# Shifting the right-hand tiles by 320 bytes, moving sums of blocks to VectorE, and three more places for split blocks in a retention + two-MLP kernel

## Chip, cores and metric

The kernel runs on one core of one Trainium2 chip. The metric is the device time of one execution in microseconds; the median of three runs of the kernel before is 931.86 us (931.78 to 934.02).

## What is computed

Attention without softmax (retention), then two MLPs, all in float32:

```python
scores = q @ k.T / sqrt(64)                       # 4 batches, 8 heads, 576 positions, 64 wide
attn = (scores * gamma_h ** (i - j) for i >= j) @ v
x = attn as [2304, 512]
h = relu(x @ w_in)                                # 512 -> 2048   (MLP 1)
y = (h * h) @ w_out                               # 2048 -> 512
g = y @ w_gate                                    # 512 -> 1536   (MLP 2)
out = (g * sigmoid(g) * (y @ w_val)) @ w_out2     # 1536 -> 512
```

## The kernel before

Products of the MLPs are made to near float32 precision with TensorE's `float32r` type: each operand is split into a high part (a ScalarE copy that rounds) and a low part (a VectorE subtraction), and `three` (lines 174 to 178) issues high x high, high x low and low x high into one bank of PSUM. Each matmul has its own weight load.

**Order of the work.** Nothing is issued while the functions run. They describe operations with an engine, an estimated duration, their dependences and a rank to a planner (`Plan`, lines 59 to 119), which simulates the engines and issues, per engine, whichever operation is ready first; among ready ones the lowest rank goes first. TensorE's operations are chained in program order. Each engine then works its instructions off in the order issued. Stores have rank -4, loads of second-MLP weights -1, the evaluation of a step of the second MLP -3 and -2, attention about 10, conversion of first-MLP weights from 100 on, of second-MLP weights from 200 on.

**Stages.**
- Start: loads, attention cells 0 to 3; while data are awaited, `fill` (line 876) repeats a matmul whose two operands are one tile of zeros, `wz`, of the pool `hp`.
- MLP 1: tokens go in five blocks (`BLOCKS`, line 27), four of 512 columns and one of 256, each over 16 slices `f` of the hidden width. Per slice, 12 matmuls make `h` in one bank (`mlp1_h`), `mlp1_act` turns it into squares and splits it (relu and high part on ScalarE, square on ScalarE in the first and last block and on VectorE in the others, low part on VectorE, line 516), and 12 matmuls one slice later add to `y` in four banks (`mlp1_y`). Attention cells for the next block lie between slices. Meanwhile weights arrive as 64-bit words and are rounded to 32 bits (`round32`): those of MLP 1 during the first block, those of MLP 2 in later blocks, and the latter are stored, already split, in DRAM (`keep`).
- MLP 2: tokens in three blocks of 768, each over 12 slices; one of the 36 steps is seven products (a Strassen-Winograd scheme over 2 x 2 blocks, `PRODUCTS`, line 42), each of 6 matmuls of 384 columns into banks `MA` and `MB` alternately (tiles `gv`), and 18 output matmuls of 512 columns (lines 806 to 808). VectorE adds a product to partial sums before its bank is free again (lines 711 to 731; `u` of L731 is the last of a step, from which the next step's first product takes its bank).

**Sums of blocks.** The scheme needs sums of blocks of the weights and of y. `convert_gv` makes four sums of 256 columns for each of 12 gate/value slices (S1 to S4, line 295, GpSimd); `fetch_x` (line 606) loads one block's y into the tile `ys`, makes four differences of 768 columns (T1 to T4, line 621, GpSimd), and `part` splits seven blocks into tiles `xc` (ScalarE copy, line 252; VectorE subtraction, line 256). There are `NX` = 9 places for `xc`, so two of the next block's seven parts fit before the running block gives places free. The splits of a block are chained one after another (`x_chain`). The first block is fetched at rank 60, the next two at rank 4.

**Weights.** A ring place holds `P` (A11, A12, A22; 768 columns, high and low part 3072 bytes apart), `S` (S1 to S4; 1024 columns, 4096 apart) or `O` (output weights).

**Addresses.** Pools on the left are stacked upward, pools with `side="right"` downward from the top, the first of them a pad of 32 bytes (line 153). In the built program every tile that TensorE reads from a left pool (`x`, `h`, `wz`, attention tiles) starts 128 bytes past a multiple of 512 but for `state` (384 past); every tile of a right pool (all weights, `xc`, the split activations `at`, the tiles of the first attention cells) starts 448 past. All sizes between are multiples of 512.

Of the kernel before, what the change touches and what calls it, by code (L numbers as in the profile page):

```python
# [10 lines left out]
F32 = mybir.dt.float32  # L11
F32R = mybir.dt.float32r
# [3 lines left out]
ALU = mybir.AluOpType  # L16
# [12 lines left out]
T2, N2 = 6, 3  # L29
HALF = T2 * C // 2  # L30
# [10 lines left out]
         ("V", 1), ("raw", 1), ("A", 2), ("q", 2), ("V", 2), ("A", 3), ("q", 3), ("V", 3)]  # L41
PRODUCTS = [("A11", "B11"), ("A12", "B21"), ("S2", "T2"), ("S1", "T1"), ("S3", "T3"), ("S4", "B22"), ("A22", "T4")]
PLAIN, SUMS = ["A11", "A12", "A22"], ["S1", "S2", "S3", "S4"]
NX, NRING = 9, 7
INSERTS = {2: (4, 10), 4: (2, 6, 10, 13)}


# [90 lines left out]
def kernel(ctx: ExitStack, tc: tile.TileContext, units, qtab, tab, w1, w2, out):  # L138
# [10 lines left out]
    nc = tc.nc  # L149
    do = Plan()  # L150

    pad = ctx.enter_context(tc.tile_pool(name="pad", bufs=1, side="right"))
    pad.tile([128, 8], F32, name="pad")
    wp = ctx.enter_context(tc.tile_pool(name="wp", bufs=NW1 - NA, side="right"))
    wstack = ExitStack()
    wa = wstack.enter_context(tc.tile_pool(name="wa", bufs=NA, side="right"))
# [91 lines left out]
    def split(get, n, out, place, rank, deps, cols=None):  # L248

        def hi():  # L250
            out["t"] = place()
            nc.scalar.copy(out=out["t"][:, 0], in_=get())

        def lo():
            t = out["t"]
            nc.vector.tensor_tensor(out=t[:, 1], in0=get(), in1=t[:, 0].bitcast(F32), op=ALU.subtract)

        h = do("ACT", 0.17 + 0.43 * n / 512, hi, deps, rank)
        return do("DVE", 0.16 + 0.53 * n / 512, lo, [h], rank)
# [13 lines left out]
    def keep(kind, i, st, n, get, rank, deps):  # L273

        out = {}

        def store():
            nc.sync.dma_start(out=w_dram[kind, i], in_=out["t"].bitcast(F32))

        l = split(get, n, out, lambda: sp.tile([128, 2, n], F32R, tag="raw1", name="cw"), rank, [*deps, place_free[1]])  # L280
        w2_saved[kind, i] = place_free[1] = do("SP", 0.4, store, [l], rank - 100, kb=n)
        return l

    def convert_gv(box, f, rank):


        st, p4 = round32(box, rank)
        a21, a11, a12, a22 = (slice(256 * i, 256 * i + 256) for i in range(4))

        def add(i, a, b, op, new=False):  # L290
            def go():
                if new:
                    st["s"] = cv.tile([128, 4, 256], F32, tag="r", name="s")
                x, y = (st["s"][:, k] if isinstance(k, int) else st["fm"][:, k] for k in (a, b))
                nc.gpsimd.tensor_tensor(out=st["s"][:, i], in0=x, in1=y, op=op)
            return go

        s = do("POOL", 0.7, add(0, a21, a22, ALU.add, True), [p4], rank)
        s = do("POOL", 0.7, add(1, 0, a11, ALU.subtract), [s], rank)
        s = do("POOL", 0.7, add(2, a11, a21, ALU.subtract), [s], rank)  # L300
        s = do("POOL", 0.7, add(3, a12, 1, ALU.subtract), [s], rank)
        l = keep("P", f, st, 768, lambda: st["fm"][:, 256:], rank, [p4])
        f_users.append(do("NONE", 0.0, lambda: None, [s, l]))
        r_users.append(keep("S", f, st, 1024, lambda: st["s"].rearrange("p a b -> p (a b)"), rank, [s, l]))
# [5 lines left out]
    late, hps_free = {}, {}  # L310
# [291 lines left out]
    XC, As, ring = {}, {}, {}  # L602
    M_op, x_op, ld_op, o_op, g_op = (Named(do, k) for k in ("M", "xc", "ld", "o2", "g2"))
    steps2 = N2 * NF2

    def fetch_x(b, rank):

        st = {}

        def load():  # L610
            st["t"] = xp.tile([128, KC + 1, T2 * C], F32, tag="x", name="ys")
            nc.sync.dma_start(out=st["t"][:, :KC], in_=y_dram[b])

        def at(name):
            if name == "T2":
                return st["t"][:, KC].rearrange("p (k n) -> p k n", k=2)
            k, h = {"B11": (0, 0), "B12": (0, 1), "B21": (2, 0), "B22": (2, 1), "T1": (0, 0), "T3": (0, 1), "T4": (2, 0)}[name]
            return st["t"][:, k:k + 2, h * HALF:h * HALF + HALF]

        def sub(o, a, c):  # L620
            return lambda: nc.gpsimd.tensor_tensor(out=at(o), in0=at(a), in1=at(c), op=ALU.subtract)

        free = [h_op[NB - 2 + b, NF1 - 1]] if b < 2 else [("ysdone", b - 2)]
        ready = {}
        ld = do("SP", 0.4, load, [*y_saved[b], *free, late["open"]], rank, kb=1536)

        def part(i, name, deps):
            n = 7 * b + i
            old = M_op[((n - NX) // 7) * NF2 + NF2 - 1, (n - NX) % 7] if n >= NX else late["open2"]
            out = {}  # L630

            def place():
                XC[b, name] = late["xc"].tile([128, 2, 2, HALF], F32R, tag="xc", name="xc")
                return XC[b, name]

            x_op[b, i] = l = split(lambda: at(name), 2 * HALF, out, place, rank, [*deps, old, *x_chain[-1:]])
            x_chain.append(l)
            return l

        b11 = part(0, "B11", [ld])  # L640
        b21 = part(1, "B21", [ld])
        t1 = do("POOL", 1.95, sub("T1", "B12", "B11"), [b11], rank)
        t2 = do("POOL", 1.95, sub("T2", "B22", "T1"), [t1], rank)
        t3 = do("POOL", 1.95, sub("T3", "B22", "B12"), [t1], rank)
        t4 = do("POOL", 1.95, sub("T4", "B21", "T2"), [t2, b21], rank)
        part(2, "T2", [t2])
        part(3, "T1", [t1])
        part(4, "T3", [t3])
        part(5, "B22", [t3])
        do.named["ysdone", b] = part(6, "T4", [t4])  # L650

    x_chain = []
# [273 lines left out]
    def convert2():  # L926
        kind, f = todo.pop(0)
        i = NW2 - 1 - len(todo)
        box = load_raw(w2, i, 0, rank=200 + i)
        (convert_gv if kind == "gv" else convert_out)(box, f, 200 + i)  # L930
# [3 lines left out]
    for j in range(NB):  # L934
        more = BLOCKS[j + 1][1] if j + 1 < NB else 0
        at = dict(zip(INSERTS[more], range(cell, cell + more))) if more else {}
        cell += more
        if not more:
            def swap():
                astack.close()  # L940
                late["tl"] = ctx.enter_context(tc.tile_pool(name="tl", bufs=1, reuse_waits="tile"))
                pgv = ctx.enter_context(tc.tile_pool(name="pgv", bufs=1, space=PSUM, reuse_waits="tile"))
                late["MA"], late["MB"], more = (pgv.tile([128, 512], F32, name=f"gv{i}") for i in range(3))
                late["more"] = [banks[0], more]
                late["tp"] = tp

            def swap2():
                wstack.close()
                for key, bufs in (("xc", NX), ("rg", 1), ("at", 2), ("tm", 1)):
                    late[key] = ctx.enter_context(tc.tile_pool(name=key, bufs=bufs, side="right", reuse_waits="tile"))  # L950

            late["open"] = do("NONE", 0.0, swap, [*(x for xs_ in x_done.values() for x in xs_), *(st_op[c] for c in range(NC))])
            late["open2"] = do("NONE", 0.0, swap2, [late["open"], y_op[NB - 1, NA - 1]])
        for f in range(NF1):
            rank = 10 + f / 100
            if f == 1:
                for _ in range(LATER.get(j, 0)):
                    convert2()
            mlp1_h(j, f)
            mlp1_act(j, f)  # L960
            if pend:
                mlp1_y(*pend)
            pend = (j, f)
            if j == 0 and f == 1:
                att_scores(n0, rank)
            c = at.get(f)
            if c is not None:
                att_out(c, rank, "IKO", deps=[relu_op[j, f]])
                if c not in LAST:
                    hps_free[(j, f + 1) if f + 1 < NF1 else (j + 1, 0)] = [st_op[c]]  # L970
                if c + 1 < NC:
                    att_scores(c + 1, rank)
                if c + 1 < NC:
                    att_load(c + 1, 40)
# [4 lines left out]
    for s in range(steps2):  # L979
        b, f = divmod(s, NF2)  # L980
        mlp2_gv(s, last_y if s == 0 else () if s == 1 else mlp2_o(s - 2))
        if s == 0:
            fetch_x(0, 60)
        if f == 1 and b + 1 < N2:
            fetch_x(b + 1, 4)
    for s in (steps2 - 2, steps2 - 1):
        for piece in mlp2_o(s):
            piece()
# [69 lines left out]
```

## Time and profile before

| | before |
|---|---|
| median of three runs | 931.86 us (931.78 to 934.02) |
| the profiled execution, its own time | 934.56 us |
| its span, first to last instruction | 932.8 us |
| TensorE busy | 909.2 us |
| VectorE busy | 593.8 us |
| ScalarE busy | 362.3 us |
| GpSimd busy | 120.5 us |
| mean granted TensorE clock | 0.994 |

The rows come from one profiled execution. Times are from the span's start. PE is TensorE (PEld its weight loads), DVE VectorE, ACT ScalarE, POOL GpSimd, SP the queue that issues all transfers. Matmuls are pipelined: the duration of one runs on after the next has begun, so the pace is read from the distance of starts. A bracket behind a row holds the engine's idle time before it and what ended it.

### The profile page before, as it was taken

What the parts mean: (1) busy time and instruction counts of PE and PEld (TensorE: products, weight loads), DVE (VectorE), ACT (ScalarE), POOL (GpSimd) and SP (SyncE); (2) the same over time, 40 slices, a digit from 0 to 9 for tenths busy, and PEclk for the clock granted to TensorE, in tenths of its full rate; (3) what the DMA queues carried; (4) which work ended last, traced back from release to release, by engine and by line L of the source; (5) the groups of instructions that cost most, each with busy time, mean ns of one, the idle gap of its engine ahead of it and who ended that gap; (6) DMA issues with size and microseconds to landing.
All of it is one profiled execution on the core that took longest, in us unless ns stands there. A gap on an engine that the chain in (4) does not pass through costs nothing.

```text
span 932.8 us, 12545 instructions
## 1 busy us (share of the span) xinstructions
PE 909.2 (97%) x4953; PEld 793.7 (85%) x4953; DVE 593.8 (64%) x872; ACT 362.3 (39%) x546; POOL 120.5 (13%) x97
## 2 busy tenths in 40 slices
PE   8899999999999999999999999998999999999997
PEld 7688879988878778878887899998999999999996
DVE  5999836457773777736455655569655557655554
ACT  3678743234541445446553222223222223322221
POOL 3210102112431312301133000003000000000000
PEclk9999999999999999999999999999999999999999
DMA  8665605337673567645436754555555455745521
GB/s 350 226 208 185 227 36 185 123 109 265 236 260 102 177 232 296 226 173 220 181 131 250 297 207 188 219 203 203 199 222 209 187 225 207 277 187 224 208 115 68
DMA packets 36634, 187.49 MB, mean 201 GB/s; under 512 B 4192, under 2 KB 5984, under 8 KB 22624
## 3 DMA queue, kind: packets, MB, share of 16 engines
q1 hardware_dynamic: 36576, 186.70, 53.7%
q8 instruction: 39, 0.64, 0.3%
q14 instruction: 19, 0.16, 0.1%
HBM read 148.93 MB, written 37.75 MB: 200 GB/s over the span
## 4 chain that ended last, share of the span: by engine, by line
PE 88%; DVE 6%; DMA 2%; ACT 2%; issue 2%; SPq 0%; ACTq 0%; DVEq 0%
PE gv L178 9%; PE gv L177 9%; PE gv L176 9%; PE acc L177 7%; PE hps L176 7%; PE acc L176 7%; PE acc L178 7%; PE hps L178 6%; PE hps L177 6%; PE acc L807 4%; PE acc L808 4%; PE acc L806 3%; DMA raw<-w 2%; PE xs L427 2%; PE sc L390 2%
## 5 line engine op out<-in xcount | busy, mean ns | idle before, releaser
L176 PE MATMUL gv<-xc,w 128*128 128x384 f32 x504 | 170.2, 338 | 5.8 <-DVE u L731 3.4
L177 PE MATMUL gv<-xc,w 128*128 128x384 f32 x504 | 171.3, 340 | 0.0
L178 PE MATMUL gv<-xc,w 128*128 128x384 f32 x504 | 171.0, 339 | 0.0
L176 PE MATMUL acc<-h,w 128*128 128x512 f32 (+1 forms) x320 | 119.5, 373 | 2.9 <-ACT yt L573 2.2
L177 PE MATMUL acc<-h,w 128*128 128x512 f32 (+1 forms) x320 | 119.5, 373 | 2.6 <-DVE h L516 2.5
L176 PE MATMUL hps<-x,w 128*128 128x512 f32 (+1 forms) x320 | 120.8, 378 | 1.0 <-ACT r L503 1.0
L177 PE MATMUL hps<-x,w 128*128 128x512 f32 (+1 forms) x320 | 119.1, 372 | 0.9 <-DVE x L452 0.9
L178 PE MATMUL hps<-x,w 128*128 128x512 f32 (+1 forms) x320 | 119.0, 372 | 0.0
L178 PE MATMUL acc<-h,w 128*128 128x512 f32 (+1 forms) x320 | 118.9, 372 | 0.0
L176 PEld LDWEIGHTS gv<-xc,w 128*128 128x128 f32 x504 | 95.5, 189 | 15.7 <-DVE u L731 4.6
L177 PEld LDWEIGHTS gv<-xc,w 128*128 128x128 f32 x504 | 95.3, 189 | 8.2
L736 ACT ACTIVATE sg<-g 128x384 f32<-128x384 f32 x72 | 37.8, 525 | 162.9 <-DVE g L728 131.5
L178 PEld LDWEIGHTS gv<-xc,w 128*128 128x128 f32 x504 | 95.4, 189 | 0.0
L503 ACT ACTIVATE r<-hps 128x512 f32<-128x512 f32 (+1 forms) x80 | 44.4, 555 | 127.1 <-PE hps L178 116.9
L516 DVE TENSOR_TENSOR h<-r,h 128x512 fp32r<-128x512 f32 (+1 forms) x80 | 55.6, 695 | 59.5 <-ACT h L513 59.0
L176 PEld LDWEIGHTS acc<-h,w 128*128 128x128 f32 x320 | 60.1, 188 | 15.9 <-ACT yt L573 2.9
L177 PEld LDWEIGHTS acc<-h,w 128*128 128x128 f32 x320 | 60.1, 188 | 15.3 <-DVE h L516 4.1
L176 PEld LDWEIGHTS hps<-x,w 128*128 128x128 f32 x320 | 60.1, 188 | 14.8 <-ACT r L503 1.9
L177 PEld LDWEIGHTS hps<-x,w 128*128 128x128 f32 x320 | 60.2, 188 | 12.1 <-DVE x L452 1.2
L178 PEld LDWEIGHTS hps<-x,w 128*128 128x128 f32 x320 | 60.1, 188 | 11.5
L178 PEld LDWEIGHTS acc<-h,w 128*128 128x128 f32 x320 | 60.1, 188 | 11.4
L509 DVE TENSOR_TENSOR r<-r 128x512 f32<-128x512 f32 (+1 forms) x48 | 33.2, 692 | 48.2 <-ACT r L503 48.2
(106 smaller groups left out, 1486.6 us busy)
## 6 DMA issues: line engine op xcount, KB each, us to landing
w<-wdS SPq DMA_DIRECT2D x36, 1024.0 KB, 5.7
raw<-w SPq DMA_DIRECT2D x34, 1024.0 KB, 4.8
w<-wdP SPq DMA_DIRECT2D x36, 768.0 KB, 5.8
w<-wdO SPq DMA_DIRECT2D x18, 1024.0 KB, 4.8
wdS<-cw SPq DMA_DIRECT2D x12, 1024.0 KB, 4.2
wdP<-cw SPq DMA_DIRECT2D x12, 768.0 KB, 3.4
qk<-units SPq DMA_DIRECT2D x14, 512.0 KB, 4.4
kv<-units SPq DMA_DIRECT2D x14, 512.0 KB, 3.9
```

The costliest lines, as they stand in the source:

```text
L176: nc.tensor.matmul(ps, lhsT=wh, rhs=xh, start=first, stop=False)
L177: nc.tensor.matmul(ps, lhsT=wh, rhs=xl, start=False, stop=False)
L178: nc.tensor.matmul(ps, lhsT=wl, rhs=xh, start=False, stop=last)
L390: nc.tensor.matmul(s[h][:, p], lhsT=A[c][r, p, 1], rhs=A[c][r, p, 0], start=True, stop=True)
L427: nc.tensor.matmul(bank("xo")[r, p], lhsT=V[c][:, p, 1, r], rhs=P[c][:, h, p], start=c in FIRST and p == 0, stop=p == NP - 1)
L503: nc.scalar.activation(out=st["r"], in_=banks[0][:, :n], func=ACTF.Relu)
L509: nc.vector.tensor_tensor(out=st["r"], in0=st["r"], in1=st["r"], op=ALU.mult)
L516: nc.vector.tensor_tensor(out=Hs[j, f][:, 1], in0=st["r"], in1=Hs[j, f][:, 0].bitcast(F32), op=ALU.subtract)
L736: nc.scalar.activation(out=t, in_=st["g"][:, r], func=ACTF.Sigmoid)
L806: nc.tensor.matmul(ps, lhsT=at[:, 0, sl], rhs=wh, start=f == 0, stop=False)
L807: nc.tensor.matmul(ps, lhsT=at[:, 0, sl], rhs=wl, start=False, stop=False)
L808: nc.tensor.matmul(ps, lhsT=at[:, 1, sl], rhs=wh, start=False, stop=f == NF2 - 1)
```

## The change

The pad grows from 32 to 352 bytes, which moves every right-hand tile down by 320 bytes, from 448 to 128 past a multiple of 512. The sums S1 to S4 and the differences T1 to T4 are issued on VectorE. The places for `xc` become twelve, three of them in a new pool `xl` on the left (at 128 past as well), nine on the right as before. All blocks are fetched at rank 60, but the last two parts of the second and third block are split at rank 4.

```diff
--- before.py
+++ after.py
@@ -41,7 +41,7 @@
          ("V", 1), ("raw", 1), ("A", 2), ("q", 2), ("V", 2), ("A", 3), ("q", 3), ("V", 3)]
 PRODUCTS = [("A11", "B11"), ("A12", "B21"), ("S2", "T2"), ("S1", "T1"), ("S3", "T3"), ("S4", "B22"), ("A22", "T4")]
 PLAIN, SUMS = ["A11", "A12", "A22"], ["S1", "S2", "S3", "S4"]
-NX, NRING = 9, 7
+NX, NXL, NRING = 12, 3, 7
 INSERTS = {2: (4, 10), 4: (2, 6, 10, 13)}
 
 
@@ -150,7 +150,7 @@
     do = Plan()
 
     pad = ctx.enter_context(tc.tile_pool(name="pad", bufs=1, side="right"))
-    pad.tile([128, 8], F32, name="pad")
+    pad.tile([128, 88], F32, name="pad")
     wp = ctx.enter_context(tc.tile_pool(name="wp", bufs=NW1 - NA, side="right"))
     wstack = ExitStack()
     wa = wstack.enter_context(tc.tile_pool(name="wa", bufs=NA, side="right"))
@@ -292,13 +292,13 @@
                 if new:
                     st["s"] = cv.tile([128, 4, 256], F32, tag="r", name="s")
                 x, y = (st["s"][:, k] if isinstance(k, int) else st["fm"][:, k] for k in (a, b))
-                nc.gpsimd.tensor_tensor(out=st["s"][:, i], in0=x, in1=y, op=op)
+                nc.vector.tensor_tensor(out=st["s"][:, i], in0=x, in1=y, op=op)
             return go
 
-        s = do("POOL", 0.7, add(0, a21, a22, ALU.add, True), [p4], rank)
-        s = do("POOL", 0.7, add(1, 0, a11, ALU.subtract), [s], rank)
-        s = do("POOL", 0.7, add(2, a11, a21, ALU.subtract), [s], rank)
-        s = do("POOL", 0.7, add(3, a12, 1, ALU.subtract), [s], rank)
+        s = do("DVE", 0.43, add(0, a21, a22, ALU.add, True), [p4], rank)
+        s = do("DVE", 0.43, add(1, 0, a11, ALU.subtract), [s], rank)
+        s = do("DVE", 0.43, add(2, a11, a21, ALU.subtract), [s], rank)
+        s = do("DVE", 0.43, add(3, a12, 1, ALU.subtract), [s], rank)
         l = keep("P", f, st, 768, lambda: st["fm"][:, 256:], rank, [p4])
         f_users.append(do("NONE", 0.0, lambda: None, [s, l]))
         r_users.append(keep("S", f, st, 1024, lambda: st["s"].rearrange("p a b -> p (a b)"), rank, [s, l]))
@@ -618,7 +618,7 @@
             return st["t"][:, k:k + 2, h * HALF:h * HALF + HALF]
 
         def sub(o, a, c):
-            return lambda: nc.gpsimd.tensor_tensor(out=at(o), in0=at(a), in1=at(c), op=ALU.subtract)
+            return lambda: nc.vector.tensor_tensor(out=at(o), in0=at(a), in1=at(c), op=ALU.subtract)
 
         free = [h_op[NB - 2 + b, NF1 - 1]] if b < 2 else [("ysdone", b - 2)]
         ready = {}
@@ -630,19 +630,20 @@
             out = {}
 
             def place():
-                XC[b, name] = late["xc"].tile([128, 2, 2, HALF], F32R, tag="xc", name="xc")
+                XC[b, name] = late["xl" if n % NX < NXL else "xc"].tile([128, 2, 2, HALF], F32R, tag="xc", name="xc")
                 return XC[b, name]
 
-            x_op[b, i] = l = split(lambda: at(name), 2 * HALF, out, place, rank, [*deps, old, *x_chain[-1:]])
+            x_op[b, i] = l = split(lambda: at(name), 2 * HALF, out, place, min(rank, 4) if b and i >= NX - 7 else rank,
+                                    [*deps, old, *x_chain[-1:]])
             x_chain.append(l)
             return l
 
         b11 = part(0, "B11", [ld])
         b21 = part(1, "B21", [ld])
-        t1 = do("POOL", 1.95, sub("T1", "B12", "B11"), [b11], rank)
-        t2 = do("POOL", 1.95, sub("T2", "B22", "T1"), [t1], rank)
-        t3 = do("POOL", 1.95, sub("T3", "B22", "B12"), [t1], rank)
-        t4 = do("POOL", 1.95, sub("T4", "B21", "T2"), [t2, b21], rank)
+        t1 = do("DVE", 0.96, sub("T1", "B12", "B11"), [b11], rank)
+        t2 = do("DVE", 0.96, sub("T2", "B22", "T1"), [t1], rank)
+        t3 = do("DVE", 0.96, sub("T3", "B22", "B12"), [t1], rank)
+        t4 = do("DVE", 0.96, sub("T4", "B21", "T2"), [t2, b21], rank)
         part(2, "T2", [t2])
         part(3, "T1", [t1])
         part(4, "T3", [t3])
@@ -938,7 +939,8 @@
         if not more:
             def swap():
                 astack.close()
-                late["tl"] = ctx.enter_context(tc.tile_pool(name="tl", bufs=1, reuse_waits="tile"))
+                for key, bufs in (("tl", 1), ("xl", NXL)):
+                    late[key] = ctx.enter_context(tc.tile_pool(name=key, bufs=bufs, reuse_waits="tile"))
                 pgv = ctx.enter_context(tc.tile_pool(name="pgv", bufs=1, space=PSUM, reuse_waits="tile"))
                 late["MA"], late["MB"], more = (pgv.tile([128, 512], F32, name=f"gv{i}") for i in range(3))
                 late["more"] = [banks[0], more]
@@ -946,7 +948,7 @@
 
             def swap2():
                 wstack.close()
-                for key, bufs in (("xc", NX), ("rg", 1), ("at", 2), ("tm", 1)):
+                for key, bufs in (("xc", NX - NXL), ("rg", 1), ("at", 2), ("tm", 1)):
                     late[key] = ctx.enter_context(tc.tile_pool(name=key, bufs=bufs, side="right", reuse_waits="tile"))
 
             late["open"] = do("NONE", 0.0, swap, [*(x for xs_ in x_done.values() for x in xs_), *(st_op[c] for c in range(NC))])
@@ -982,7 +984,7 @@
         if s == 0:
             fetch_x(0, 60)
         if f == 1 and b + 1 < N2:
-            fetch_x(b + 1, 4)
+            fetch_x(b + 1, 60)
     for s in (steps2 - 2, steps2 - 1):
         for piece in mlp2_o(s):
             piece()
```

## Rows read from the trace of the kernel before

**Rows 1.** The page: the span, and busy time of the engines (share, instructions).
```profile
span 932.8 us, 12545 instructions
PE 909.2 (97%) x4953; PEld 793.7 (85%) x4953; DVE 593.8 (64%) x872; ACT 362.3 (39%) x546; POOL 120.5 (13%) x97
```
**Rows 2.** The page: the chain that ended last, by engine.
```profile
PE 88%; DVE 6%; DMA 2%; ACT 2%; issue 2%; SPq 0%; ACTq 0%; DVEq 0%
```
**Rows 3.** Groups by line and shape: count, busy us, mean ns, idle before.
```profile
L176 PE MATMUL gv<-xc,w 128*128 128x384 f32 x504 | 170.2, 338 | 5.8 <-DVE u L731 3.4 <-DVE g L711 1.2 <-DVE u L715 1.1
L176 PE MATMUL hps<-x,w 128*128 128x512 f32 x256 | 102.7, 401 | 1.0 <-ACT r L503 1.0
...
L806 PE MATMUL acc<-w,at 128*128 128x512 f32 x144 | 56.3, 391 | 0.0
```
**Rows 4.** Timeline of TensorE in MLP 1 (start, duration): 34 matmuls, first and last.
```profile
300.16 0.40 PE L176 MATMUL hps<-x,w 128*128 128x512 f32 x1
...
307.86 0.39 PE L176 MATMUL hps<-x,w 128*128 128x512 f32 x1
```
**Rows 5.** Timeline of TensorE in MLP 2, starts of runs of matmuls.
```profile
801.38 0.39 PE L806 MATMUL gv<-w,at 128*128 128x512 f32 x1
...
802.77 0.33 PE L176 MATMUL gv<-xc,w 128*128 128x384 f32 x1
...
803.82 0.33 PE L176 MATMUL gv<-xc,w 128*128 128x384 f32 x1
...
804.86 0.39 PE L806 MATMUL acc<-w,at 128*128 128x512 f32 x1
...
807.32 0.33 PE L176 MATMUL gv<-xc,w 128*128 128x384 f32 x1
...
808.38 0.39 PE L806 MATMUL acc<-w,at 128*128 128x512 f32 x1
...
906.75 0.33 PE L176 MATMUL gv<-xc,w 128*128 128x384 f32 x1
```
**Rows 6.** Timeline of TensorE at the start: runs of idle matmuls, merged.
```profile
7.08 2.60 PE L879 MATMUL hps<-wz 128*128 128x512 f32 x10
...
9.51 2.66 PE L879 MATMUL hps<-wz 128*128 128x512 f32 x11
```
**Rows 7.** Stretches: length, busy us (count) of PE, PEld, DVE, ACT, POOL, PEclk, DMA.
```profile
500.00:550.00 50.00, 46.55 (x235) 42.84 (x234) 33.84 (x55) 14.22 (x26) 8.71 (x4) 0.97 0.67 250
515.50:518.90 3.40, 3.25 (x10) 3.25 (x11) 1.92 (x5) 0.00 (x0) 0.00 (x0) 0.50 0.53 207
652.00:655.40 3.40, 3.40 (x12) 3.11 (x11) 2.93 (x6) 1.78 (x3) 0.00 (x0) 0.51 0.27 102
```
**Rows 8.** Timeline, 643 to 651 us: GpSimd, VectorE and TensorE.
```profile
643.06 6.07 POOL L621 TENSOR_TENSOR ys<-ys 128x768 f32<-128x768 f32 x3 [131.39 <-DVE xc L256]
...
643.17 2.16 DVE L718 TENSOR_TENSOR g<-u,m 128x384 f32<-128x384 f32 x1 [0.24 <-ACT m L706]
...
650.93 0.44 PE L176 MATMUL gv<-xc,w 128*128 128x384 f32 x1 [2.33 <-DVE u L731]
```
**Rows 9.** Groups by line and shape, of VectorE and GpSimd.
```profile
L621 POOL TENSOR_TENSOR ys<-ys 128x768 f32<-128x768 f32 x12 | 25.6, 2152 | 180.0 <-DVE xc L256 155.6 <-PE acc L178 24.1
...
L256 DVE TENSOR_TENSOR at<-g,at 128x768 fp32r<-128x768 f32 x36 | 34.5, 957 | 27.4 <-ACT at L252 27.3
...
L718 DVE TENSOR_TENSOR g<-u,m 128x384 f32<-128x384 f32 x36 | 21.7, 602 | 38.7 <-ACT m L706 38.7
...
L509 DVE TENSOR_TENSOR r<-r 128x256 f32<-128x256 f32 x16 | 6.8, 426 | 18.4 <-ACT r L503 18.4
```
**Rows 10.** A stretch of the first block of MLP 1, columns as in rows 7.
```profile
60.00:100.00 40.00, 40.00 (x209) 32.77 (x208) 35.51 (x44) 32.30 (x41) 2.99 (x2) 1.00 0.59 207
```
**Rows 11.** Timeline of a later block: a low half of h, and its first reader.
```profile
305.17 0.69 DVE L516 TENSOR_TENSOR h<-r,h 128x512 fp32r<-128x512 f32 x1 [0.69 <-ACT h L513]
...
308.56 0.40 PE L176 MATMUL acc<-h,w 128*128 128x512 f32 x1
```

## The prediction

> **What bounds the kernel now.** I read the page first, then the groups by line, then single matmuls in the timeline. The page shows TensorE busy for 97% of the span, VectorE 64%, GpSimd 13% [rows 1], and the chain that ended last lies on TensorE for 88% [rows 2]. The reader should see that only two things can move the end: the pace of matmuls that follow each other without a gap, and the few gaps. The groups give the counts: 3 x 504 = 1512 products of 384 columns in MLP 2 and, in MLP 1, 6 x 256 = 1536 matmuls of 512 columns (three lines for h, three for y; one shown); the output matmuls of MLP 2 are 36 steps x 18 = 648, of which one line has 144 in the four `acc` banks [rows 3]. Their mean durations overlap and are no pace, so I take the pace from distances of starts.
>
> In MLP 1, 33 distances lie between 300.16 and 307.86 us: 7.70/33 = 0.2333 us for 512 columns [rows 4]. In MLP 2, six output matmuls take 801.38 to 802.77, 0.2317 each. Nine steps take 802.77 to 906.75, 11.553 each; a step is 42 products and 18 output matmuls, so a product takes (11.553 - 18 x 0.2317)/42 = 0.1758 us. The products are not alike: the six from 803.82 to 804.86 (weights whose high and low parts lie 3072 bytes apart) take 0.1733 each, the six from 807.32 to 808.38 (4096 apart) 0.1767 [rows 5]. The two kinds have the same shape, the same engine and the same moving operands; what differs is where the weights lie. So an address can cost pace.
>
> **Where operands lie.** In MLP 1 the weights are 448 bytes past a multiple of 512 and x and h 128 past; in MLP 2 both operands are 448 past. Only the idle matmuls of the start (one tile read as both operands) have everything 128 past. They are the one sample of the new layout: eleven from 9.51 us end after 2.66 us, and one of that shape lasts 0.39, so they are 2.27/10 = 0.2270 apart. Just before, right after a pause, ten are (2.60 - 0.39)/9 = 0.2456 apart [rows 4, 6]. The settled row is what long streams resemble, so I take 0.2270; the other is the bad end.
>
> **Part 1, the pad.** It adds 320 bytes below the top, so weights, xc and the activations go from 448 to 128; tiles on the left stay. It costs no instruction.
> - MLP 1, 512 columns: 1536 x (0.2333 - 0.2270) = 9.7 us. Bounds: by the unsettled row 1536 x (0.2333 - 0.2456), 18.9 us lost; a gain beyond the settled row is excluded by no row, but none shows it.
> - MLP 2 outputs: 648 x (0.2317 - 0.2270) = 3.0 us. Bounds: 0 (both operands have equal offsets already) to 3.0; a loss by the same unsettled row would be 9.0.
> - MLP 2 products: I take the best product of the same shape, 0.1733: 1512 x 0.0025 = 3.8 us. Bounds: nothing; or 0.2270 scaled to 384 columns, 0.1703, which is 8.3 us.
> - The 256-column block and the attention: 0.2270/2 = 0.1135 for 256 columns, which I set to no change; `state` keeps its place.
> Sum 16.5 us.
>
> Here a rule speaks against the change. The trace shows a pace that differs between products of one shape by 0.0034 us with the addresses of the weights [rows 5]. The Trainium skill, page "TensorE: Matmul & The Clock Gate", Part 2, says that the moving operand and the weight load have read ports of their own, so that loading the next weights takes no bandwidth from the running matmul, and gives about 0.2157 us between matmuls of 512 columns. By that page the address term would be nil; its figure is not what this trace shows (0.2333), and the trace decides.
>
> **Part 2, sums on VectorE.** It takes 48 sums of 256 columns and 12 of 768 off GpSimd. On VectorE a two-operand 256-column instruction takes 0.426 us and a 768-column one 0.957: 48 x 0.426 = 20.4 us and 12 x 0.957 = 11.5 us of work [rows 9]. GpSimd needed 2.15 us for each 768-column one, and while it works VectorE stands still: from 643.06 three of them run 6.07 us, and an addition (L718) that takes 0.602 on average takes 2.16; TensorE then starves for 2.33 us [rows 8, 9]. Right after it the clock falls to 0.51 (1.2 GHz) for 3.4 us, which at half pace loses 1.7 us; the same happened at 515.5 to 518.9 after gaps at the start of MLP 2 [rows 7].
> - At 643 us: 2.33 + 1.7 go, and four sums in VectorE's order cost perhaps 0.3: 3.7 us. Bounds: 0 (the sums hold up the same L731) to 4.0.
> - At 500 to 520 us: TensorE misses 3.45 of 50 us and 1.7 by the clock [rows 7]. Part of it is first steps that wait on their own banks, and VectorE now gets three more splits there (part 3) and four sums, 6.7 us. I take 1.5; bounds -2 to 4.
> - MLP 1: the 20.4 us lie beside TensorE. In a block, the low half of h starts on VectorE at 305.17 and ends 0.69 later, and the matmuls that read it start at 308.56: 2.7 us to spare [rows 11], against 0.43 for a sum that gets ahead of it. Cost nothing; if the spare time were gone, 48 x 0.426 = 20.4 us. Behind each sum on VectorE's queue stand squares and low halves of h, and the weight splits that free the conversion buffers; these start earlier, as four sums take 1.7 us.
> - In the first block VectorE is busy 35.51 of 40 us converting weights [rows 10]. A TensorE faster by 2.7% still leaves it below full; cost 0, at worst the 2.4 us that this block (a quarter of the 512-column work) would gain.
>
> **Part 3, twelve places and ranks.** The tile of y is loaded by one SP instruction; rank 60 for 4 moves it past nothing, as stores (-4) and ring loads (-1) go first either way and no rank between is left on SP or GpSimd. With nine places two of the next block's seven parts can be split early, with twelve five. That moves three splits of 0.957 and their ACT copies from a block's end to its start; counted above. The last two keep rank 4, so nothing waits longer for them. Cost nothing: what hides it is VectorE's free third; without it, three splits would be 2.9 us a block.
>
> **Sum.** 16.5 + 3.7 + 1.5 = 21.7 us. The profiled execution took 934.56 us (span 932.8 and 1.76 around it), 2.7 above the median of 931.86. So 934.56 - 21.7 = 912.9 there, and 931.86 - 21.7 = 910.2 as a median.
>
> **Rivals.**
> - Address helps MLP 1 alone (MLP 2's operands already share one offset, and its outputs still run at 0.2317): 9.7 + 5.2 = 14.9, 917 us. For it: equal offsets bought nothing there. Against: the settled fill has equal offsets too and is faster.
> - The address does nothing, by whatever makes the fill fast (one tile, one bank, the same weights each time), or since the ports are separate: 5.2 us of gaps remain, 926.7. Against it: the two kinds of product [rows 5]. This is what the page of the skill named above would give.
> - VectorE falls behind: half of the moved sums delay a low half of h by their full 0.43 us, 24 x 0.426 = 10.2 us: 920.4. It decides once the 2.7 us to spare are used up; for it stands the 89% of the first block, though no sum falls there.
> - Slower: with x, h and weights on one offset the two reads of TensorE meet, and MLP 1 runs at the unsettled 0.2456: 18.9 us lost, less the 5.2 of the gaps, MLP 2 unchanged: 945.6. It turns the sign from a pace of 0.2333 + 5.2/1536 = 0.2367 on. For it: the first ten fills. Against: they settle at the same addresses.
> That the change doesn't do what it says is hardly possible for a pad: the offset of every right tile follows from it.
>
> **How the numbers follow.** Full forecast 0.62, MLP 1 alone 0.14, no address effect 0.12, VectorE behind 0.06, slower 0.06. The likeliest gives 910.2. Downward, 4.5 (products at 0.1703) and 2.5 (all of the gap at 500 to 520) reach 903; upward, the range takes in MLP 1 alone (917), VectorE behind (920.4) and a full forecast that loses the first block's 2.4, the 1.5 at 500 and the 3.7 at 643 (918), with the 2 and more that the bound below nothing at 500 allows on top of MLP 1 alone: 922. Left out are the last two signs, 0.18. A measurement of this kernel tells some 0.3% (2.8 us) from no change. Every case but the slower one is faster by more than that; from the case without address effect I set 0.07 aside for gaps that don't close. So faster 0.87, same 0.07, slower 0.06.
>
> **What would show it.** Right: 512-column matmuls 0.227 apart in MLP 1 and in the outputs, a step of MLP 2 of 42 x 0.1733 + 18 x 0.2270 = 11.36 us, no VectorE instruction over 1.4 us between 630 and 655, full clock at the second block. GpSimd should show only its attention work, VectorE some 30 us more, less what it no longer stands still. Wrong: MLP 1 still at 0.233, a step still at 11.55, or waits of matmuls for the low half of h that add up to more than a few us.

## The result, and the profile after the change

| | before | after |
|---|---|---|
| median of four runs | 931.82 us (930.94 to 934.02) | 918.51 us (916.75 to 919.21) |
| ratio, with its 95% interval | | 0.9851 [0.9829, 0.9873] |
| the profiled execution, its own time | 934.56 us | 918.46 us |

The change takes 13.3 us off the median. Forecast were 21.7 (910.2 us, range 903 to 922): the right sign and inside the range, but 8 us too hopeful. The page after, its span and its engines' busy time:

```profile
span 916.7 us, 12530 instructions
PE 898.4 (98%) x4953; PEld 791.8 (86%) x4953; DVE 597.6 (65%) x932; ACT 360.9 (39%) x546; POOL 45.4 (5%) x37
```

GpSimd has lost its 60 sums. VectorE has 60 instructions more but only 3.8 us more of busy time [rows 1]: what it got in work it no longer spends standing still.

**MLP 1.** The timeline of TensorE, the first and the last start of 34 matmuls without a gap, once with 512 columns and once in the 256-column block:

```profile
290.11 0.39 PE L177 MATMUL hps<-x,w 128*128 128x512 f32 x1
...
297.59 0.39 PE L177 MATMUL acc<-h,w 128*128 128x512 f32 x1
...
176.05 0.28 PE L177 MATMUL hps<-x,w 128*128 128x256 f32 x1
...
180.01 0.28 PE L177 MATMUL hps<-x,w 128*128 128x256 f32 x1
```

512 columns: 7.48/33 = 0.2267 us, against 0.2333 in [rows 4]. 256 columns: 3.96/33 = 0.1200. 34 matmuls of this block before the change, which the prediction did not use:

```profile
176.99 0.28 PE L177 MATMUL hps<-x,w 128*128 128x256 f32 x1
...
180.75 0.28 PE L177 MATMUL hps<-x,w 128*128 128x256 f32 x1
```

3.76/33 = 0.1139. So the pad makes the wide matmuls 2.8% faster and the narrow ones 5% slower.

**MLP 2.** Starts of three steps (15th, 27th and 36th):

```profile
647.98 0.33 PE L176 MATMUL gv<-xc,w 128*128 128x384 f32 x1
...
786.64 0.33 PE L176 MATMUL gv<-xc,w 128*128 128x384 f32 x1
...
890.62 0.33 PE L176 MATMUL gv<-xc,w 128*128 128x384 f32 x1
```

The last nine steps take 103.98 us, 11.553 each: to the nanosecond what they took before [rows 5]. The address gained nothing here; both operands of MLP 2 lay 448 past a multiple of 512 before and lie 128 past now, so the difference between them stayed 0. What did change is the gaps. MLP 2 now starts 9.5 us earlier, so the stretches that answer [rows 7, 8] lie earlier too (columns as in rows 7):

```profile
490.49:540.49 50.00, 47.68 (x247) 43.73 (x247) 38.22 (x64) 16.70 (x30) 0.00 (x0) 1.00 0.66 256
624.00:650.00 26.00, 26.00 (x137) 24.12 (x136) 23.24 (x39) 10.28 (x19) 0.00 (x0) 1.00 0.73 264
```

No gap and no half clock at the second block; 2.32 us missing at the start of MLP 2 instead of 3.45, at full clock. The low half of h (groups by line), before:

```profile
L516 DVE TENSOR_TENSOR h<-r,h 128x512 fp32r<-128x512 f32 x64 | 47.2, 737 | 53.8 <-ACT h L513 53.3
```

The same after the change, and below it the sums in their new place (of the 48 sums of weights one half is shown):

```profile
L516 DVE TENSOR_TENSOR h<-r,h 128x512 fp32r<-128x512 f32 x64 | 44.2, 691 | 47.3 <-ACT h L513 46.4 <-PE acc L178 0.6
...
L621 DVE TENSOR_TENSOR ys<-ys 128x768 f32<-128x768 f32 x12 | 11.3, 954 | 0.1
L295 DVE TENSOR_TENSOR s<-f 128x256 f32<-128x256 f32 x24 | 10.1, 421 | 0.2
```

**Where the time of the profiled executions went.** The first product of MLP 2 starts at 497.25 before and 487.74 after, the last step 409.50 and 402.88 later, and the rest is equal (first before, then after):

```profile
497.25 0.34 PE L176 MATMUL gv<-xc,w 128*128 128x384 f32 x1
```
```profile
30.13 0.48 PE L176 MATMUL hps<-x,w 128*128 128x512 f32 x1
...
487.74 0.33 PE L176 MATMUL gv<-xc,w 128*128 128x384 f32 x1
```

So 9.5 us come from the time ahead of MLP 2 and 6.6 from its gaps and half clock, 16.1 in all. Added up over all distances in MLP 1 without idle time, the wide matmuls went from 353.0 to 344.0 us: 9.0, less than the 1536 x 0.0066 = 10.1 of settled ones. The narrow ones went from 44.3 to 46.3 and give 2.0 back. What else lies in MLP 1, attention cells and waits, went from 68.1 to 67.3, 0.8. The last 1.7 is a start of MLP 1 at 30.13 that was at 31.85 in that one execution before the change. The other runs with a profile start it at 29.6 to 30.5 whatever was changed, so this belongs to the execution, and is part of why it stood 2.7 us above its median. Without it 14.4 are left.

### The profile page after: what moved, and what is told of

Read it like the earlier page. It is cut to its first block, busy times and chain, and to the rows that moved or that the text cites. A ratio compares the mean times of both kernels' runs of the same rounds, so it can differ in the third digit from the quotient of the medians.

```text
span 916.7 us, 12530 instructions
## 1 busy us (share of the span) xinstructions
PE 898.4 (98%) x4953; PEld 791.8 (86%) x4953; DVE 597.6 (65%) x932; ACT 360.9 (39%) x546; POOL 45.4 (5%) x37
## 4 chain that ended last, share of the span: by engine, by line
PE 90%; DMA 3%; DVE 3%; ACT 2%; issue 1%; SPq 0%; ACTq 0%
PE gv L178 9%; PE gv L177 9%; PE gv L176 9%; PE hps L176 7%; PE acc L177 7%; PE acc L176 7%; PE acc L178 7%; PE hps L177 7%; PE hps L178 6%; PE acc L808 4%; PE acc L809 4%; PE acc L807 4%; DMA raw<-w 2%; PE xs L427 2%; PE sc L390 2%; PE xs L417 1%
## 5 line engine op out<-in xcount | busy, mean ns | idle before, releaser
L178 PE MATMUL gv<-xc,w 128*128 128x384 f32 x504 | 170.1, 338 | 0.0
L176 PE MATMUL acc<-h,w 128*128 128x512 f32 (+1 forms) x320 | 118.4, 370 | 3.2 <-ACT yt L573 2.3
L177 PE MATMUL acc<-h,w 128*128 128x512 f32 (+1 forms) x320 | 118.2, 369 | 0.7 <-DVE h L516 0.7
L178 PE MATMUL hps<-x,w 128*128 128x512 f32 (+1 forms) x320 | 117.8, 368 | 0.0
L178 PE MATMUL acc<-h,w 128*128 128x512 f32 (+1 forms) x320 | 117.7, 368 | 0.0
L178 PEld LDWEIGHTS gv<-xc,w 128*128 128x128 f32 x504 | 94.7, 188 | 0.0
L516 DVE TENSOR_TENSOR h<-r,h 128x512 fp32r<-128x512 f32 (+1 forms) x80 | 52.1, 652 | 53.5 <-ACT h L513 52.6
L176 PEld LDWEIGHTS hps<-x,w 128*128 128x128 f32 x320 | 60.2, 188 | 14.4 <-ACT r L503 2.8
L178 PEld LDWEIGHTS hps<-x,w 128*128 128x128 f32 x320 | 60.3, 188 | 10.2
L178 PEld LDWEIGHTS acc<-h,w 128*128 128x128 f32 x320 | 60.3, 189 | 9.9
L707 ACT COPY m<-gv 128x384 f32<-128x384 f32 x72 | 34.4, 477 | 78.6 <-PE gv L178 78.6
```

Of the source, the lines that this page charges most:

```text
L176: nc.tensor.matmul(ps, lhsT=wh, rhs=xh, start=first, stop=False)
L177: nc.tensor.matmul(ps, lhsT=wh, rhs=xl, start=False, stop=False)
L178: nc.tensor.matmul(ps, lhsT=wl, rhs=xh, start=False, stop=last)
L516: nc.vector.tensor_tensor(out=Hs[j, f][:, 1], in0=st["r"], in1=Hs[j, f][:, 0].bitcast(F32), op=ALU.subtract)
L707: nc.scalar.copy(out=st[name], in_=late[bank][:, :HALF])
```

## Experiments

Each run is compared with runs of the kernel before on the same chip. A difference in us is that of the two medians; the ratio with its interval is formed from all runs and can differ from it by 0.1%.

**1. Taking the change apart.** `e1_pad_only`: the kernel before with

```diff
-    pad.tile([128, 8], F32, name="pad")
+    pad.tile([128, 88], F32, name="pad")
```

> The kernel before with the pad alone (88 for 8 floats). Both theories of the address: matmuls of 512 columns in MLP 1 go from 0.2333 to 0.227 us (9 to 10 us less) and the 256-column block from 0.114 to 0.120 (2.2 us more), MLP 2 keeps 0.2324 and a mean product of 0.1755; the gaps at the second block of MLP 2 with their half clock stay. So 7 us less: 924 to 926. If the new order of VectorE, not the address, were what made the pace, nothing would change: 931 to 932.

Measured 927.19 us, 0.9949 [0.9933, 0.9965]: 5.6 us less, and 1.2 us above the expected range. MLP 1 has the new pace with the engines' old order (33 distances, 0.2267 each; the narrow block runs at 0.120):

```profile
291.51 0.39 PE L176 MATMUL acc<-h,w 128*128 128x512 f32 x1
...
298.99 0.39 PE L176 MATMUL acc<-h,w 128*128 128x512 f32 x1
```

The gap at the second block stays:

```profile
640.00:650.00 10.00, 7.62 (x33) 6.85 (x32) 9.33 (x11) 1.84 (x3) 6.00 (x4) 0.85 0.54 207
```

TensorE misses 2.4 of these 10 us, and its clock is 0.85 in the mean; GpSimd works 6.0 of them.

`e2_no_pad`: the changed kernel with the pad back at 8 floats.

> The changed kernel with the pad of before (8 floats): sums on VectorE, twelve places and ranks alone. The theory that the gaps of MLP 2 come from VectorE standing still beside GpSimd: no instruction of VectorE over 1.4 us after 640 us, no half clock in MLP 2, 5 to 7 us less than before: 925 to 927; MLP 1 keeps 0.2333 and 0.114. Rival, that the gain is all in the address: 931 to 932. The three places on the left lie at another difference to the weights than the nine on the right here; if the difference matters for 384 columns, their products run at another pace than 0.1755.

Measured 924.41 us, 0.9920 [0.9903, 0.9937]: 8.3 us less, and 0.6 us below the expected range. The two parts make 13.9 us, and together they were 13.3: they add, and the sums with their places and ranks are probably the larger one (their intervals overlap slightly). The stretch of the gap is full:

```profile
640.00:660.00 20.00, 20.00 (x106) 18.57 (x105) 17.18 (x29) 8.17 (x15) 0.00 (x0) 1.00 0.67 230
```

`e4_pool_sums`: the changed kernel, all sums on GpSimd (`nc.vector.tensor_tensor` back to `nc.gpsimd.tensor_tensor` at lines 295 and 621, the planner's engine and durations with them).

> The changed kernel with all sums back on GpSimd; pad, twelve places and ranks stay. If the sums' engine closed the gaps: VectorE instructions of over 1.4 us beside GpSimd's differences of blocks come back, with waits of TensorE in MLP 2 of 3 us or more and perhaps a stretch at half clock: 921 to 925. If the twelve places did it (differences run earlier, when nobody is in a hurry): 917 to 919.

Measured 928.76 us, 0.9965 [0.9953, 0.9976], slower than expected. Places and ranks without the sums on VectorE don't close the gap; against `e1_pad_only` (0.9949) they gain nothing at all. What they are worth once the sums are on VectorE no run shows. Timelines of GpSimd, VectorE and TensorE:

```profile
629.13 6.05 POOL L621 TENSOR_TENSOR ys<-ys 128x768 f32<-128x768 f32 x3 [123.61 <-DVE xc L256]
...
633.55 2.05 DVE L744 TENSOR_TENSOR g<-m,g 128x384 f32<-128x384 f32 x1
...
636.95 0.44 PE L176 MATMUL gv<-xc,w 128*128 128x384 f32 x1 [3.04 <-ACT m L707]
```

An elementwise multiplication (L744) that takes 0.558 on average in the changed kernel takes 2.05 beside the three differences, ScalarE's split behind it (line 252) starts late, the copy m behind that too, and TensorE waits 3.04 us.

`g3_weights_pool`: the changed kernel with only the 48 sums of weights back on GpSimd (line 295).

> The changed kernel with the 48 sums of weights (S1 to S4) back on GpSimd, the 12 differences of y on VectorE. If the gain of the sums is that of MLP 2 alone: 917 to 919, with no long instruction of VectorE after 640 us. If the sums of weights earn something too (VectorE no longer stands still in MLP 1, waits for the low half of h): 920 to 924, with waits of TensorE on the low half of h of 2 us or more against 0.7 in the changed kernel.

Measured 921.08 us, 0.9889 [0.9867, 0.9912]: 10.2 us less than before, where the changed kernel has 13.3 and `e4_pool_sums` 4.0. So the twelve differences of y are worth some 6 us and the 48 sums of weights some 3. TensorE's waits (in total, times, longest), in this run:

```profile
PE acc L177 <- DVE h L516: 2.7, 5, 1.2
```

and in the changed kernel:

```profile
PE acc L177 <- DVE h L516: 0.7, 3, 0.3
```

These waits make 2 of the 3 us; the rest isn't located.

**2. What about the address counts.** `e3_all_448`: the changed kernel with the pad of before on the right, and on the left

```diff
+    padl = ctx.enter_context(tc.tile_pool(name="padl", bufs=1))
+    padl.tile([128, 80], F32, name="padl")
```

> The changed kernel with the pad of before and 320 bytes more at the bottom of the left side, so that all operands lie 448 bytes past a multiple of 512 and none 128. Theory A, the difference between the two operands' offsets counts: MLP 1 at 0.227 for 512 columns and 0.120 for 256, total as the changed kernel, 917 to 919. Theory B, 128 past is what counts: 0.2333 and 0.114, MLP 2 unchanged, total 925 to 927.

Measured 917.21 us, 0.9843 [0.9826, 0.9860]: as fast as the changed kernel, with nothing 128 past. Its timeline in MLP 1:

```profile
290.12 0.39 PE L178 MATMUL hps<-x,w 128*128 128x512 f32 x1
...
297.60 0.39 PE L178 MATMUL acc<-h,w 128*128 128x512 f32 x1
```

Two lines were added, so L178 is the first of the three matmuls here. 33 distances are 7.48 us, 0.2267 each. What counts is the difference between the two operands' addresses, not where they lie.

`f1_d256` (pad of 24 floats, difference 256) and `f2_d64` (72 floats, difference 64):

> The changed kernel with a pad of 24 floats: right-hand tiles 384 past a multiple of 512, left ones 128 past, difference 256 in MLP 1 (0 in the changed kernel, 320 before). Theory A1: any difference other than 0 gives the pace of before, 0.2333 for 512 columns and 0.114 for 256. Theory A2: the pace changes from difference to difference, and 256 may be better or worse than both for either width.

> The changed kernel with a pad of 72 floats: difference 64 in MLP 1. Theory A1: 0.2333 and 0.114, as at 320. Theory A2: another pair of paces. If 512 columns run at 0.227 and 256 columns at 0.114 at once, this is a better pad than both, by 2 us.

Single runs: 917.92 and 924.22 us. The first in MLP 1:

```profile
290.22 0.39 PE L178 MATMUL hps<-x,w 128*128 128x512 f32 x1
...
297.70 0.39 PE L178 MATMUL acc<-h,w 128*128 128x512 f32 x1
```

and the second, wide and narrow:

```profile
290.18 0.39 PE L176 MATMUL acc<-h,w 128*128 128x512 f32 x1
...
297.88 0.40 PE L176 MATMUL hps<-x,w 128*128 128x512 f32 x1
...
176.08 0.28 PE L177 MATMUL acc<-h,w 128*128 128x256 f32 x1
...
179.82 0.28 PE L177 MATMUL acc<-h,w 128*128 128x256 f32 x1
```

At 256 it is 7.48/33 = 0.2267, as at 0. At 64 it is 7.70/33 = 0.2333 and 3.74/33 = 0.1133, as at 320 before. Theory A1 fell, and of A2 only half came: two differences other than 0 gave two answers, but these are the two paces already known. The four differences fit a reading modulo 128: 0 and 256 leave 0, 64 and 320 leave 64. Modulo 256 would fit them as well; other differences (16, 32, 128, 192) weren't tried in MLP 1.

`f3_block256`: the 256-column block alone gets the other remainder, by 192 bytes ahead of its x and, in the same way, its h:

```diff
-        X[j] = xp.tile([128, KC, 2, BLOCKS[j][1] * C], F32R, tag="x", name="x")
+        n = BLOCKS[j][1] * C
+        o = 48 if n == 256 else 0
+        t = xp.tile([128, o + KC * 2 * n], F32R, tag="x", name="x")
+        X[j] = t[:, o:].rearrange("p (k a n) -> p k a n", k=KC, a=2)
```

> The changed kernel with the x and h of the 256-column block alone moved up by 192 bytes, so that weights less moving operand is 320 there, as before the change, and 0 in the other blocks. Theory of the difference: 256 columns back from 0.1197 to 0.114, 384 of them, 2.2 us less: 915 to 917, nothing else changes. Rival (what slowed the 256-column block is the new order of VectorE or the faster blocks around it): 0.1197 stays, 917 to 919.

Measured 915.21 us, 0.9829 [0.9808, 0.9851]. 33 distances of the block:

```profile
184.10 0.28 PE L177 MATMUL hps<-x,w 128*128 128x256 f32 x1
...
187.84 0.28 PE L177 MATMUL hps<-x,w 128*128 128x256 f32 x1
```

3.74/33 = 0.1133: the 5% that the change had cost this block are back, and its order of VectorE and its neighbours are those of the changed kernel.

**3. Why MLP 2 gained nothing.** `f4_interleave` lays S1 to S4 and the output weights out in blocks, each with its low part right behind its high part (one of several places in the code):

```diff
-    ring[kind, s] = pool.tile([128, 2, w], F32R, tag="w", name="w2")
+    shape = {"P": [128, 2, 768], "S": [128, 4, 2, 256], "O": [128, 2, 2, 512]}[kind]
+    ring[kind, s] = pool.tile(shape, F32R, tag="w", name="w2")
```

> The changed kernel with the high and low parts of the sums S1 to S4 laid 1024 bytes apart instead of 4096, and those of the output weights 2048 apart instead of 4096 (as x and h are in MLP 1). Theory that MLP 2 is held by the distance between the high and low part of its weights: the 864 products with S run at 0.1733 as those with P do, instead of 0.1767, 3 us less; if the output matmuls also reach 0.227, another 3.2: 912 to 916. Rival, that the number of the product or its bank of PSUM makes the difference: paces stay, 917 to 919.

Measured 917.30 us, 0.9850 [0.9831, 0.9870]: no change from the distance of the parts. The six products with S2 still take 1.06 us, 0.1767 each:

```profile
787.91 0.33 PE L176 MATMUL gv<-xc,w 128*128 128x384 f32 x1
...
788.97 0.39 PE L812 MATMUL acc<-w,at 128*128 128x512 f32 x1
```

The theory that I had read into the two kinds of product fell.

The changed kernel's MLP 1 right behind an attention cell suggests another (timeline of TensorE):

```profile
235.99 0.40 PE L177 MATMUL hps<-x,w 128*128 128x512 f32 x1
...
238.32 0.39 PE L178 MATMUL hps<-x,w 128*128 128x512 f32 x1
238.55 0.39 PE L176 MATMUL acc<-h,w 128*128 128x512 f32 x1
...
241.04 0.39 PE L178 MATMUL acc<-h,w 128*128 128x512 f32 x1
```

The first ten distances are 2.33/10 = 0.233, the eleven from 238.55 on 2.49/11 = 0.2264. This stream needs about ten matmuls of one length to fall into its pace (to settle). The outputs of MLP 2 come in runs of three or six. `g1_one_run` makes them one run of 18 (calls `other(0)` to `other(5)` moved together):

```diff
         product(1, "MB", [("c12", s - 1)])
...
-        other(1)
+        for i in range(T2):
+            other(i)
         product(2, "MA", [m1])
```

> The changed kernel with the 18 output matmuls of a step of MLP 2 in one run after the second product, instead of six runs of three between the products. Theory of settling (the fast pace comes only after about ten matmuls of one length in a row; in the changed kernel the output runs of three to six end before that): within a run the first ten lie some 0.232 apart and the last eight 0.227, and the long run of products settles to one pace too. Rival (the outputs are held by something of their own, such as the change of bank or where their weights lie): 0.232 from first to last. The time itself may get worse by waits on the two banks, which the pieces hide now: 915 to 935.

Single run, 943.89 us, beyond the expected range. Inside one run of outputs (the last row is the product behind it):

```profile
806.20 0.39 PE L803 MATMUL acc<-w,at 128*128 128x512 f32 x1
...
808.51 0.39 PE L804 MATMUL acc<-w,at 128*128 128x512 f32 x1
...
810.32 0.33 PE L176 MATMUL gv<-xc,w 128*128 128x384 f32 x1
```

The first ten distances are 2.31/10 = 0.231, the last eight 1.81/8 = 0.226. The outputs can run at the fast pace; their runs were never long enough. The run changes its bank every three matmuls and settles all the same, so a change of bank isn't what holds them. The order costs far more than it gives, though, as the pieces had hidden the way of a bank through VectorE (TensorE's waits):

```profile
PE gv L176 <- DVE u L732: 24.3, 35, 1.1
```

`g2_mlp2_64` gives MLP 2 the other remainder: pools of 64 bytes ahead of `xl`, `xc`, `rg` and `at` (16 floats each), so that xc and the activations end up 64 from the weights, modulo 128.

> The changed kernel with xc and the split activations moved by 64 bytes, so that in MLP 2 too the two operands differ by 64 modulo 128, MLP 1 as changed. If the difference modulo 128 sets only the settled pace, short runs don't care: output matmuls stay at 0.232 and products at 0.1755, 917 to 919. If it acts on every matmul, outputs go up by 0.004 or more and products to another mean: 3 us or more slower or faster.

Measured 915.18 us, 0.9823 [0.9794, 0.9852]. Starts of the 15th and the 36th step:

```profile
646.66 0.34 PE L176 MATMUL gv<-xc,w 128*128 128x384 f32 x1
...
888.04 0.34 PE L176 MATMUL gv<-xc,w 128*128 128x384 f32 x1
```

21 steps take 241.38 us here and 242.64 after the change (647.98 to 890.62): 0.06 a step, 2.2 us in 36. Neither alternative came as worded: by the mean of all distances in MLP 2 the outputs stay at 0.232 (0.2321 and 0.2325), and the products go from 0.1756 to 0.1741. So the remainder acts on short runs of products as well, and for them 64 is the better one.

**4. A better version.** `h1_both` joins `f3_block256` and `g2_mlp2_64`.

> The changed kernel with the 256-column block moved by 192 bytes (f3_block256) and xc and the split activations moved by 64 (g2_mlp2_64). Theory that each stage has its own best difference modulo 128 and that they add: 256 columns at 0.1147, products at a mean of 0.1741, MLP 1 else at 0.227: 2.0 and 2.1 us less than the changed kernel, 912 to 915. Rival, that the two runs gained by chance of the other waits: 915 to 918.

Measured 913.75 us, 0.9810 [0.9796, 0.9823]: 18.1 us below before, against 13.3 of the change. Starts in the narrow block, and of the 27th and the 36th step:

```profile
175.89 0.28 PE L177 MATMUL hps<-x,w 128*128 128x256 f32 x1
...
179.63 0.28 PE L177 MATMUL acc<-h,w 128*128 128x256 f32 x1
...
781.90 0.34 PE L176 MATMUL gv<-xc,w 128*128 128x384 f32 x1
...
885.54 0.34 PE L176 MATMUL gv<-xc,w 128*128 128x384 f32 x1
```

The narrow block runs at 3.74/33 = 0.1133, and a step takes 103.64/9 = 11.516 against 11.553. Both paces are there at once, and the two gains add within the noise: each stage has its own remainder.

## Why the prediction was right and wrong

- **MLP 1, 512 columns: right.** 9.7 us by 0.2333 less 0.2270; measured 0.2267 once settled, and 9.0 us. The fill was a fair sample here, since runs of 24 and more settle, and since its two operands are one tile, difference 0. That everything there lies 128 past, by which I chose it, doesn't matter (`e3_all_448`). That it was the address, and not the order of engines, `e1_pad_only` and `e3_all_448` show.
- **MLP 2 outputs, 3.0 us: wrong.** The pad couldn't give them anything: both operands lay 448 past before and 128 past after, difference 0 both times, as the lower bound said; a step still at 11.55 is what the prediction had named as a sign of being wrong. What kept them at 0.232 was the length of their runs. The step that failed is "the settled row is what long streams resemble" where there are no long streams. Six output matmuls in a row are shorter than the settling that [rows 6] itself showed; I used the unsettled row as a bad end for MLP 1 and not as the rate of short runs. `g1_one_run` shows both paces inside one run.
- **MLP 2 products, 3.8 us: wrong, with a false witness.** I put the two paces of [rows 5] down to where the weights lie, and called all else equal; the neighbours in the stream were not. `f4_interleave` moved their low parts and the pace stayed. The slow six follow three 512-column matmuls, the fast six follow other products: a place in the order, not an address. In `g1_one_run` the six products behind the long run of outputs take 810.32 to 811.39, 0.178 each, and later ones settle at 0.173, those with S among them.
- **The 256-column block, set to no change: wrong.** 0.1139 to 0.1200, 2.0 us lost in the profiled pair. Half of the fill's pace was taken as its price and not its own starts; 0.1139 would have shown that it already ran at that half and had more to lose than to gain.
- **The gap at 643 us, 3.7 us, and that at 500, 1.5: right in kind.** The second block of MLP 2 went from 142.81 to 138.67 us, 4.1 less, and the first from 139.60 to 137.13, 2.5 less: 6.6 against 5.2. In the first block 1.1 us is idle time; the other 1.4 is the half clock at 515.5, which `e1_pad_only` doesn't have either, though its sums are on GpSimd and TensorE has the same three gaps there (1.1 to 1.2 us each; its first block takes 138.20). So that part differs between executions, and the sums get no credit for it. The signs named for the second block came: full clock, and no VectorE instruction over 1.4 us between 630 and 655. `e1_pad_only` and `e2_no_pad` put the gap at the second block to the sums with their places, and `e4_pool_sums` to the sums' engine rather than the places.
- **The sums in MLP 1, nothing: too low.** They cost nothing, as predicted, but `g3_weights_pool` shows about 3 us of gain that I hadn't claimed. The profiled pair doesn't show it: of the time of attention cells and waits in MLP 1 it has 0.8 us less, and this time differs by 2 us between executions (65.2 in `e3_all_448`, 67.3 in the changed kernel, with the same sums on VectorE).
- **The sum: inside the range, but by a rival and not by the likeliest case.** 6.8 us that the sum had for MLP 2 didn't come, and 2.0 that it left out were lost in the narrow block; 1.4 more in the gaps and 0.8 in MLP 1 made up a little of it. The range holds the result because it took in "MLP 1 alone". Its upper end, 922, is 1.5 above what its terms give (917 + 1.5 + 2 = 920.5); the measured 918.5 lies under both.
- **Rivals.** The one that happened is "address helps MLP 1 alone" (0.14, 917 us), with 2.0 us taken back by the narrow block. Of the slower rival this much came: with both operands on one remainder the narrow matmuls lose. By the Trainium skill, page "TensorE: Matmul & The Clock Gate", Part 2, loading the next weights takes no read bandwidth from the running matmul; the rival without an address effect (0.12) drew on that. It didn't happen: with the same instructions and order, 512 columns take 0.2267 or 0.2333 us by the difference between the addresses of the two operands alone. Whether the weight load is what takes the time, no run shows.
- **VectorE behind: no.** Waits on the low half of h fell from 2.5 to 0.7 us.

## What to carry to other kernels

Read the pace of each shape from distances of starts, in the run length in which the kernel has it: a sample from a long stream says nothing for runs shorter than its settling. When two kinds of an instruction differ, list everything in which they differ (the neighbours too) before putting it down to one. A pad that moves both operands alike changes nothing here; look at the difference of their addresses, stage by stage. And where VectorE feeds TensorE, work beside it on GpSimd was not free: moving it added 3.8 us to VectorE's busy time, as VectorE no longer stood still.

## What the runs showed of the hardware that was not expected

- Two paces of `float32r` matmuls in MLP 1, set by the difference of the operands' addresses: 0.2267 and 0.2333 us for 512 columns, and the other way round, 0.1200 and 0.1133, for 256. Differences of 0 and 256 bytes give the one, 64 and 320 the other. Why, no run shows.
- About ten matmuls of one length pass before the fast pace of 512 columns sets in, after an attention cell as in a run of outputs.
- Beside GpSimd's differences of 768 columns, two-operand instructions of VectorE on 384 columns took up to 2.16 us before the change (L718, mean 0.602 [rows 8, 9]) and 2.05 in `e4_pool_sums` (L744, 0.558 in the changed kernel).
- After the gaps in MLP 2 the granted clock stood at 0.5 (1.2 GHz) for 3.4 us in the profiled execution before the change [rows 7]; after it MLP 2 had no such stretch until the end of the work. Gaps of one size don't always bring it: `e1_pad_only` ran on at full clock after the same three gaps at the start of MLP 2, and has such a stretch in MLP 1 instead, at 275.0 us behind a gap of 1.39.
